# A fused attention and MLP kernel on one core: its 1722 jobs emitted in another order, with the PSUM banks dealt anew

## The chip, the cores and the metric

The kernel runs on one core of one Trainium2 chip. The metric is the device time of one execution, in microseconds (us), as the median of several runs. Inputs and outputs lie in the chip's memory; the kernel reads about 38 MB and writes about 17 MB there, most of it its own scratch.

## What is computed

One input `x` of 2048 tokens by 512 columns goes through a layer norm, and three things are added: `x` itself, an attention over four segments of 512 tokens with a memory carried from segment to segment, and a two-layer MLP on the normed tokens.

```python
xn = layernorm(x)
for s in range(4):                       # 32 heads of 16 columns; q, k, v = xn @ wq, wk, wv
    p = softmax(qs @ ks.T / 4 + mask)    # causal inside a segment
    a_dot = p @ vs
    a_mem = (phi(qs) @ M) / (phi(qs) @ z + 1e-6)      # phi(t) = t + 1 if t > 0 else exp(t)
    out_s = g * a_mem + (1 - g) * a_dot               # g = sigmoid(beta), one number per head
    M += phi(ks).T @ vs;  z += sum(phi(ks))
y = gelu(layernorm(xn) @ w1 + b1) @ w2 + b2           # 512 -> 1792 -> 512
return x + concat(out_s) @ wo + y
```

## The kernel before, in words

Matrices are split into a high and a low float16 half, and a product is made of three matmuls (high by high, high by low, low by high); the attention weights stay in float32. The work is cut into small jobs, each a short Python function that issues a few instructions on one to four engines. Sixteen units `i` (four segments times four groups of eight heads) and sixteen half-blocks `j` of the MLP run through them:

- front: `X` loads and norms a pair of token tiles (`ln`, L535, L549), `Xt` turns it on TensorE and splits it (`ln_out`, L564 to L568), `W` is a filler of two matmuls on the identity (`warm`, L500) that nobody reads, and `wl`, `wm`, `wf`, `ws` load the weights, measure their size (L353 on ScalarE, L382 as a trace on TensorE with L384 on VectorE), make power-of-two scales from that (L396, L414 and small VectorE steps) and split them (L447 and L448, or L450, L452, L454). `Cb` writes a row of ratios out of the norms (L527).
- `T` projects q or k of a unit (L586) and `V` the values (L586); the halves go through scratch memory to the layout that the scores need (`Tr`, L646).
- `M` makes scores and their row maxima (L740 on TensorE, L747 on VectorE), ten jobs a unit. `R` (`m_row`, L753) turns the 128x32 table of maxima `mc` on TensorE, ScalarE and VectorE split it into `mhl` (L755, L756), and SyncE's queue writes it to `md` (L758) and reads it back as two more rows of `qst` (`Rr`, L763).
- `S` makes the scores once more with the maxima subtracted by those rows (L782), ScalarE takes the exponential (L789) and GpSimd masks it (`Sg`, L803); `pv` and `PV` multiply by the values (L816); `O` divides (six steps).
- `N`, `K`, `Z`, `Q`, `Qt` keep the memory (L651, L717, L681, L696), `D` is the first MLP product (L586 with w1, L884), `G` the gelu (L891), `H` its split (L901, L903, L905), `e` the second product (L931, L935), `out` the output product (L951, L953), `st` the store (L864), `A` the loads of the accumulators (L909, L913).

TensorE works in three tilings: the whole 128x128 array (most jobs), two halves of 64 rows that work side by side (`M` and `S`), and four strips of 32 columns (`pv`, `PV`, `K`). `R` is a float32 transposition whose stationary operand `mc` has 32 columns, so its matmul is written with a 128x32 tile too.

What sets the order: nothing is scheduled at run time or by the compiler. A string of letters, `ORDER`, names for every step the stream from which the next job is taken, and the jobs are issued in that order; each engine works off its own instructions in the order in which they were issued, and waits by semaphores for what it needs. A second string, `BANKS`, names which of the eight PSUM banks each product is written to:

```python
banks = iter("".join(BANKS))
def dense():
    return dps.tile([P, 512], F32, name="dense" + next(banks), bufs=1)

for c in "".join(ORDER):
    key = next(todo[NAMES.index(c)])
```

A bank is taken again only when the last reader of what it held is done. Both strings were written by a search outside the kernel.

## Time and profile before

| | us |
|---|---|
| median of 3 runs | 690.41 (689.52 to 692.23) |
| span of the profiled execution, first to last instruction | 690.7 |
| TensorE busy, share of the span | 680.1, 98% |
| VectorE busy | 498.9, 72% |
| ScalarE busy | 471.4, 68% |
| GpSimd busy | 346.4, 50% |
| first matmul, end of the last matmul, after the span's start | 1.4, 687.0 |

The profiled execution's span and the median of the runs differ by 0.3 us. A timeline row gives a start, a duration, the engine, the line and operation, and the tiles as out<-in; `x6` are six instructions of the same kind, so the time from the start of one row to the start of the next is what the row cost its engine. Matmuls overlap, so a row's own duration is longer than that.

### The profile page before, as it was taken

To read this page: it belongs to the slowest core of one execution; us is meant where nothing else is said; L and a number is where in the kernel's file an instruction comes from. 1 tells how busy PE (TensorE), PEld (TensorE's weight loads), DVE (VectorE), ACT (ScalarE), POOL (GpSimd) and SP (SyncE) were. 2 spreads that over 40 slices of the span, in tenths; PEclk is the share of its full clock that TensorE was granted. 3 is DMA by queue.
4 is the path that set the end of the run, shared out by engine and by line. 5 is a ranking of instruction groups with operands and counts; after the bars stand their busy time and mean duration, and the time that the engine had idled before them with its cause. 6 is when DMAs were issued, how large, how long until landed. Compare 5 with 4: busy or idle time off the path is not lost.

```text
span 690.7 us, 15732 instructions
## 1 busy us (share of the span) xinstructions
PE 680.1 (98%) x5787; PEld 394.6 (57%) x5787; DVE 498.9 (72%) x1613; ACT 471.4 (68%) x877; POOL 346.4 (50%) x574
## 2 busy tenths in 40 slices
PE   8999999999999999999999999999999999999997
PEld 6764565656644565665555555566565446565543
DVE  5789888986796669676695875878468565787622
ACT  4578898897765578578836838556956554777960
POOL 5576587663525444373545344534372425365652
PEclk9999999999999999999999999999999999999999
DMA  9788433203320342312222133231411222420101
GB/s 267 230 199 218 113 91 105 79 2 91 81 49 16 87 108 55 95 47 72 70 70 57 31 79 86 57 85 39 99 35 56 69 65 61 107 65 2 33 1 61
DMA packets 52889, 55.83 MB, mean 81 GB/s; under 512 B 4990, under 2 KB 41868, under 8 KB 52812
## 3 DMA queue, kind: packets, MB, share of 16 engines
q1 hardware_dynamic: 50508, 50.64, 26.8%
q0 software_dynamic: 2304, 4.20, 3.8%
q8 instruction: 45, 0.74, 0.5%
q14 instruction: 32, 0.26, 0.1%
HBM read 37.77 MB, written 17.05 MB: 79 GB/s over the span
## 4 chain that ended last, share of the span: by engine, by line
PE 87%; DVE 8%; DMA 2%; issue 1%; SPq 1%; POOL 1%; ACT 0%; DVEq 0%
PE dense L586 35%; PE dense L931 20%; PE dense L816 10%; PE dense L951 6%; PE dense L782 6%; PE dense L740 5%; DVE dense L747 4%; PE dense L681 2%; PE dense L696 1%; DVE mc L747 1%; PE dense L564 1%; DMA pt<-in_A_wv_dram 1%; PE dense L651 1%; DMA qst<-md 1%; PE dense L382 0%
## 5 line engine op out<-in xcount | busy, mean ns | idle before, releaser
L747 DVE CUSTOM_DVE_ANT_0 dense<-dense,mask 128x384 f32<-128x384 f32 (+3 forms) x512 | 234.0, 528 | 33.9 <-PE dense L740 33.6
L789 ACT ACTIVATE pt<-dense,qkcs 128x512 f32<-128x512 f32 (+1 forms) x384 | 204.2, 628 | 46.3 <-PE dense L782 46.2
L931 PE MATMUL dense<-w2s,hT 128*128 128x512 f16 x672 | 166.3, 380 | 0.2 <-DVE hT L884 0.2
L586 PE MATMUL dense<-xnT,w1s 128*128 128x256 f16 x1344 | 160.2, 273 | 0.3 <-DVE mc L747 0.3
L803 POOL TENSOR_SCALAR_AFFINE_SELECT pt<-pt 128x256 f32<-128x256 f32 x256 | 99.4, 422 | 108.2 <-ACT pt L789 107.8
L586 PEld LDWEIGHTS <-w1s 128*128 128x128 f16 x1344 | 129.6, 98 | 29.1 <-issue 6.2
L905 POOL TENSOR_TENSOR hT<-hh,hT 128x512 f16<-128x512 f32 x64 | 67.6, 1057 | 83.6 <-ACT hT L903 70.4
L931 PEld LDWEIGHTS <-hT 128*128 128x128 f16 x672 | 61.3, 98 | 68.6 <-issue 13.4
L816 PE MATMUL dense<-pt,vt 128*32 128x512 f32 (+3 forms) x1024 | 78.0, 436 | 0.0
L747 DVE DVE_READ_ACCUMULATOR2_ANT mc<- 128x1 f32 x512 | 74.2, 145 | 0.0
L884 DVE SCALAR_TENSOR_TENSOR hT<-dense,sc,cb 128x512 f32<-128x512 f32 x64 | 43.5, 680 | 33.8 <-PE dense L586 25.2
L847 POOL TENSOR_TENSOR nN<-nN,oT 128x512 f32<-128x512 f32 x16 | 20.9, 1308 | 73.9 <-DVE oT L663 73.9
L901 POOL TENSOR_SCALAR hh<-hT,sc 128x512 f32<-128x512 f32 x64 | 42.5, 664 | 24.1 <-ACT hT L891 15.5
L816 PEld LDWEIGHTS dense<-pt,vt 128*32 128x32 f32 x1024 | 31.1, 109 | 40.7 <-issue 29.4
L782 PE MATMUL dense<-qst,kst 50*128 50x384 f16 (+3 forms) x512 | 52.1, 299 | 1.8 <-DMA qst<-md 1.8
L740 PE MATMUL dense<-kst,qst 48*128 48x384 f16 (+3 forms) x512 | 52.2, 298 | 0.0
L891 ACT ACTIVATE hT<-hT,b1t 128x256 f32<-128x256 f32 x112 | 47.0, 496 | 5.0 <-DVE hT L884 4.6
L903 ACT ACTIVATE hT<-hh 128x512 f16<-128x512 f32 x64 | 37.3, 583 | 14.9 <-POOL hh L901 14.9
L951 PE MATMUL dense<-wos,oT 128*128 128x512 f16 (+2 forms) x204 | 44.0, 367 | 0.8 <-DVE acc L953 0.7
L586 PE MATMUL dense<-xnT,wks 128*128 128x512 f16 (+1 forms) x252 | 44.5, 329 | 0.2 <-DVE mc L747 0.2
L586 PE MATMUL dense<-xnT,wqs 128*128 128x512 f16 (+1 forms) x252 | 44.2, 329 | 0.1
L586 PE MATMUL dense<-wvs,xnT 128*128 128x512 f16 x192 | 43.9, 379 | 0.1
(227 smaller groups left out, 832.0 us busy)
## 6 DMA issues: line engine op xcount, KB each, us to landing
kst<-kd SPq DMA_DIRECT2D x32, 192.0 KB
qst<-qd SPq DMA_DIRECT2D x32, 192.0 KB
qd<-hl SPq DMA_DIRECT2D x36, 128.0 KB
kd<-hl SPq DMA_DIRECT2D x33, 128.0 KB
acc<-in_A_x_dram SPq DMA_DIRECT2D x16, 256.0 KB
acc<-in_B_b_dram POOLq DMA_DIRECT2D x16, 256.0 KB, 4.2
out_dram<-acc SPq DMA_DIRECT2D x15, 256.0 KB
xt<-in_A_x_dram SPq DMA_DIRECT2D x14, 256.0 KB
```

The source lines that it names most:

```text
L586: T.matmul(p, ws(k, a), xs(k, b), start=i == 0, stop=i == 3 * KT - 1)
L740: T.matmul(p[:, o:o + n], stk[i, 0][r, t, P * qb:P * qb + P], stk[i, 1][r, t, :n], start=True, stop=True)
L747: V.tensor_tensor_reduce(p[:, o:o + n], p[:, o:o + n], mask[:, 512 - n:], 1.0, -3e38, OP.add, OP.max, mc[i][:, 4 * b + t, qb:qb + 1])
L782: T.matmul(p[:, o:o + n], stk[i, 1][r, t, P * kb:P * kb + P], stk[i, 0][r, t, P * kb:], start=True, stop=True)
L789: A.activation(pt[i, 4 * b + t][:, OFF[kb]:OFF[kb] + n], p[:, c:c + n], AF.Exp, scale=qkcs[:, 1, i % NG:i % NG + 1])
L803: G.affine_select(v, v, pattern=[[0, 2], [1, P]], compare_op=OP.is_ge, fill=0.0, base=0, channel_multiplier=-1)
L816: T.matmul(p[32 * c:32 * c + 32, P * kb:], vt[s, kb][:, 4 * g + c, 16 * odd:16 * odd + 32], pt[i, 2 * c + odd][:, OFF[kb]:OFF[kb] + LEN[kb ...
L884: V.scalar_tensor_tensor(hz[:, f0:f + 1, :], p[:, :256 * n].rearrange("p (f c) -> p f c", f=n), col(CG + fh), cbt[hf].unsqueeze(1).to_broa ...
L891: A.activation(hz[:, f, :], hz[:, f, :], AF.Gelu_apprx_tanh, bias=b1t[:, fo:fo + 1])
L905: G.tensor_tensor(hT[:, z, 1, :], hht[j, c], hT[:, z, 0, :], op=OP.subtract)
L931: T.matmul(p, t[:, u, P * a:P * a + P], w2s[:, fo, v, :], start=fi == 0 and n == 0, stop=fi == FH - 1 and n == 2)
L951: T.matmul(p[:, c], o[:, u, P * b:P * b + P], wos[:, g, v, c], start=i == 0, stop=i == 3 * NG - 1)
```

## The change

`ORDER` and `BANKS` are replaced; not a job is added, removed or altered. The strings have the same lengths (1722 jobs, 964 products that take a bank). The new order comes from a search that charges every change of TensorE's tiling.

```diff
 ORDER = (
-    "auhhwhhhlkhhkhhbth6xc6khldlhhie$hfhhhhkjhx6f78$hhahhv$rg7%%8%k8%h8bR8cs8mRde8i&ff9m9gj9n&!n&#y&z((CA)9*(CD+(+2"
...
+    "ahukhhhkhtbhhlslclhdeh6ihh6khjfh6hahfhhwkhh$h$v87$7%bcrhxmk%gh8g8ih%d%eRfmfR888$&8nxhCnj&9&9y&z()A((*DC!((+XDX"
...
 BANKS = (
-    "01234567012345670123460123647013654701542670546173250641732570641257106457106457103645120365412306524306512430"
...
+    "00000000000001223334444455670011233467346675146370254136702541736254130625413062541306254730564273526743502764"
...
 )
```

What that does to the engines' queues is shown at three places.

The first is TensorE where unit 0's maxima are turned (L753, the job `R`). In the old program the rows around it are these (L586 is the MLP's first product, L931 its second, L414 the sum of a weight's size; the many equal rows between are left out):

```order
L586 MATMUL dense_960<-xnT,w1s 128x256
...
L931 LDWEIGHTS hT_126
L931 MATMUL dense_858<-w2s,hT_126 128x512
...
L753 MATMUL dense_1001<-ident,mc 32x128
...
L414 MATMUL dense_1021<-am,ones 128x4
```

And in the new one (L717 is the memory's product, job `K`, in strips of 32 columns; L740 the scores of unit 1, in halves of 64 rows):

```order
L931 MATMUL dense_845<-w2s,hT_126 128x512
L717 MATMUL dense_996<-vt_84,pkn 32x32 x4
L717 MATMUL dense_996<-vt_85,pkn 32x32 x4
L717 MATMUL dense_996<-vt_86,pkn 32x32 x4
L717 MATMUL dense_996<-vt_87,pkn 32x32 x4
L753 MATMUL dense_1014<-ident,mc 32x128
L740 LDWEIGHTS qst_89
L740 MATMUL dense_1030<-kst_91,qst_89 128x512
```

`R` stood inside work on the whole array, and now stands between a job in column strips and one in row halves. Of the sixteen `R`, eight now follow a job in column strips and one a job in row halves; before, all sixteen followed a job on the whole array. Counted over the whole of both programs, by the tile that each matmul is written with, the tiling changes 298 times before and 282 times after. With `R` counted as work on the whole array it changes 266 times before and 270 times after.

The second place is SyncE's queue around the same step: `md` is the write and the read-back of the maxima, `oT` the last two pieces of w2, `rc` and `ame` pieces of w1. Before:

```order
L310 DMA rc<-in_B_w_dram 128x4x128
L310 DMA ame<-in_B_w_dram 128x4x128
L646 DMA kst_91<-kd_93 48x4x512 x2
L646 DMA qst_89<-qd_95 48x4x512 x2
L758 DMA md_96<-mhl 32x2x128
L312 DMA oT<-in_B_w_dram 128x512 x2
L763 DMA qst_88<-md_96 2x2048 x2
```

After:

```order
L646 DMA kst_91<-kd_93 48x4x512 x2
L646 DMA qst_89<-qd_95 48x4x512 x2
L310 DMA rc<-in_B_w_dram 128x4x128
L310 DMA ame<-in_B_w_dram 128x4x128
L312 DMA oT<-in_B_w_dram 128x512 x2
L758 DMA md_96<-mhl 32x2x128
L763 DMA qst_88<-md_96 2x2048 x2
```

The half megabyte for `oT` was issued between the write of the maxima and their read-back, and is now issued ahead of the write.

The third place is VectorE at the front, where it splits the first weights (L448), sums the trace of wv (L384) and takes the sums of the second pair of token tiles (L474, L475). Before:

```order
L448 SCALAR_TENSOR_TENSOR wks<-wks,qksc 128x512
L384 SCALAR_TENSOR_TENSOR dense_217,am<-dense_217,ident 128x128
L978 COPY gr<-zr 128x32
L981 TENSOR_TENSOR zr<-zr,half 128x8 x4
L982 TENSOR_REDUCE bet<-zr 128x4
L388 TENSOR_SCALAR dense_316<-dense_316 128x1
L392 TENSOR_SCALAR sc<-dense_316 128x1 x2
L975 COPY b1t<-dense_321 128x14
L448 SCALAR_TENSOR_TENSOR wqs<-wqs,qksc 128x512
L448 SCALAR_TENSOR_TENSOR wvs<-wvs,sc 128x512 x2
L448 SCALAR_TENSOR_TENSOR wvs<-pt,sc,wvs 128x512 x2
L474 BN_STATS st<-nN 128x6
```

After:

```order
L384 SCALAR_TENSOR_TENSOR dense_273,am<-dense_273,ident 128x128
L978 COPY gr<-zr 128x32
L981 TENSOR_TENSOR zr<-zr,half 128x8 x4
L982 TENSOR_REDUCE bet<-zr 128x4
L448 SCALAR_TENSOR_TENSOR wks<-wks,qksc 128x512
L388 TENSOR_SCALAR dense_307<-dense_307 128x1
L392 TENSOR_SCALAR sc<-dense_307 128x1 x2
L448 SCALAR_TENSOR_TENSOR wqs<-wqs,qksc 128x512
L448 SCALAR_TENSOR_TENSOR wvs<-wvs,sc 128x512
L474 BN_STATS st<-nN 128x6
L475 BN_AGGR ag<-st 128x2
L474 BN_STATS st<-nD 128x6
```

The low half of wk now stands behind the trace of wv, and the sums of the second pair of tiles stand ahead of three of the four low halves of wv. At the same time the fillers before TensorE's first other matmul go from 26 matmuls to 24, that first matmul is the ratio row (L527) where it was the trace of wv (L382), and SyncE loads wk and wq ahead of wv.

## The prediction, on record before the changed kernel ran

> **What bounds the kernel now.** I read the page first, then the windows by stage, then who TensorE waited for, and last TensorE's timeline. The page's first lines and three windows (us of the stretch, then busy us of each engine, granted clock, DMA share) settle where the time is:

> ```profile
> span 690.7 us, 15732 instructions
> PE 680.1 (98%) x5787; PEld 394.6 (57%) x5787; DVE 498.9 (72%) x1613; ACT 471.4 (68%) x877; POOL 346.4 (50%) x574
> 75.00:200.00 125.00, 124.75 (x1183) 74.85 (x1182) 105.56 (x334) 106.12 (x199) 74.95 (x127) 1.00 0.29 72
> 200.00:400.00 200.00, 199.73 (x1770) 115.42 (x1772) 148.50 (x490) 132.84 (x246) 93.92 (x163) 1.00 0.24 62
> 400.00:660.00 260.00, 259.84 (x2116) 145.61 (x2109) 177.76 (x577) 172.97 (x321) 121.76 (x197) 1.00 0.25 62
> ```

> From 75 to 660 us TensorE is idle 0.25 + 0.27 + 0.16 = 0.7 us. The other engines have room (VectorE's fullest stretch is 105.56 of 125). Since the same matmuls run after the change, three things alone can move the end: what TensorE pays between matmuls when its tiling changes, the idle time at both ends, and new waits in the middle. The view of TensorE's waits (total, times, longest) has one that is longer than a start or a tail, in the first scores of unit 0:

> ```profile
> PE dense L782 <- DMA qst<-md: 1.8, 2, 1.3
> ```

> **Term 1, the changes of tiling.** Their price is read from starts on TensorE's timeline (start, duration, then what):

> ```profile
> 60.76 0.81 PE L931 MATMUL dense<-w2s,hT 128*128 128x512 f16 x3
> 61.41 0.27 PE L753 MATMUL dense<-ident,mc 128*32 128x128 f32 x1
> 61.52 0.81 PE L931 MATMUL dense<-w2s,hT 128*128 128x512 f16 x3
> 62.16 0.28 PE L414 MATMUL dense<-am,ones 128*128 128x4 f32 x2
> 62.30 1.46 PE L931 MATMUL dense<-w2s,hT 128*128 128x512 f16 x6
> 63.60 0.60 PE L651 MATMUL dense<-ident,phk 128*128 128x128 f32 x4
> 64.03 0.81 PE L931 MATMUL dense<-w2s,hT 128*128 128x512 f16 x3
> 64.78 0.61 PE L740 MATMUL dense<-kst,qst 48*128 48x512 f16 x6
> 65.32 2.12 PE L931 MATMUL dense<-w2s,hT 128*128 128x512 f16 x9
> 67.84 0.39 PE L782 MATMUL dense<-qst,kst 50*128 50x512 f16 x1 [0.41 <-DMA qst<-md]
> 69.57 0.39 PE L782 MATMUL dense<-qst,kst 50*128 50x512 f16 x1 [1.35 <-DMA qst<-md]
> ```

> Three L931 cost 0.65 us (60.76 to 61.41) where more work on the whole array follows, 0.217 us each, and 0.75 us (64.03 to 64.78) where row halves follow: a change costs 0.75 - 0.65 = 0.10 us, 0.095 with the trace's finer digits. Column strips are no different:

> ```profile
> 320.33 1.46 PE L931 MATMUL dense<-w2s,hT 128*128 128x512 f16 x6
> 321.72 2.14 PE L816 MATMUL dense<-pt,vt 128*32 128x512 f32 x24
> ```

> Six L931 need 6 x 0.217 = 1.30 us and took 1.39, so 0.09 us into strips. But the first three rows above show more: the transposition of the maxima (L753, written as 128*32) begins 0.65 us after the three L931, with nothing added, and the L931 behind it begins 0.11 us later, which is what other 128-column float32 transpositions cost (four L651 in 63.60 to 64.03, 0.108 each). L753 costs no change: to TensorE it is work on the whole array. Counted so, the changes go from 266 to 270, not from 298 to 282, and term 1 is +4 x 0.095 = +0.4 us. The new order puts `R` behind column strips eight times, a neighbourhood that the old trace does not show. Should strips pass into `R` and on to the whole array free of charge, eight changes vanish, and 262 stay: -4 x 0.095 = -0.4 us. I take +0.4, since the rows that are there all treat `R` as whole-array work; ends -1.5 and +0.4.

> [...]

> **Term 2, the first scores of unit 0.** In the rows above the nine L931 end at 65.32 + 9 x 0.217 + 0.095 = 67.36. The first L782 starts 0.48 us late, its partner, which would follow within 0.01 us, 1.73 us after it: 2.2 us lost. The chain of waits and SyncE's queue say why:

> ```profile
> 62.72 2.63 DMA md<-mhl
> 65.67 3.85 DMA qst<-md
> ```

> ```profile
> 62.72 0.30 SPq L758 DMA_DIRECT2D md<-mhl  x1
> 63.07 2.00 SPq L312 DMA_DIRECT2D oT<-in_B_w_dram  x2
> 65.36 0.57 SPq L763 DMA_DIRECT2D qst<-md  x2
> ```

> The read-back of 16 KB took 3.85 us with 512 KB of w2 just in front of it. After the change that half megabyte goes out before the write of the maxima. Against this, TensorE has less to do meanwhile. From L753 to the place of the first L782 it had 67.36 - 61.41 = 5.95 us. Now it has, from the rows above, L753 0.11, a change 0.095, two M jobs with the change out of them 0.54 (64.78 to 65.32), six `e` jobs at 0.65, L414 0.14, N 0.43, a change and one M 0.31: 5.53 us. A later round, with the queue quiet, shows what is enough:

> ```profile
> 408.05 0.27 PE L753 MATMUL dense<-ident,mc 128*32 128x128 f32 x1
> 413.45 0.82 PE L782 MATMUL dense<-qst,kst 50*128 50x512 f16 x8
> ```

> There 5.40 us sufficed without a wait. At 60 us weights still flow, so I leave 0.8 us of the 2.2: -1.4 us. Ends: -2.2 (nothing left), and +0.5 (0.4 us of cover gone, the transfers no faster).

> **Term 3, the front.** Four idle stretches before 36 us carry names on TensorE's timeline; the first is the cold start, which stays.

> ```profile
> 1.42 5.73 PE L500 MATMUL dense<-ident 128*128 128x256 bf16 x26 [1.42 <-POOL ident masks.py:199]
> 7.58 0.63 PE L382 MATMUL dense<-wvs 128*128 128x128 bf16 x8 [0.42 <-DMA wvs<-in_A_wv_dram]
> 11.66 0.40 PE L382 MATMUL dense<-pt 128*128 128x128 bf16 x4 [0.48 <-DMA pt<-in_A_wv_dram]
> 12.39 0.40 PE L382 MATMUL dense<-pt 128*128 128x128 bf16 x4 [0.34 <-DMA pt<-in_A_wv_dram]
> 13.95 1.48 PE L586 MATMUL dense<-xnT,wks 128*128 128x256 f16 x12
> 16.18 2.75 PE L586 MATMUL dense<-wvs,xnT 128*128 128x512 f16 x12
> 33.14 1.47 PE L586 MATMUL dense<-xnT,w1s 128*128 128x256 f16 x12
> 35.61 0.38 PE L414 MATMUL dense<-am,ones 128*128 128x1 f32 x2 [1.00 <-DVE dense L384]
> ```

> They idle 0.42 + 0.48 + 0.34 + 1.00 = 2.2 us, and with the last matmul's tail that runs out ahead of each, about 0.2 us, 3.0 us are lost. In the new order the waits for wv should go, as it has 24 filler matmuls, the first pair's turn and seven more filler jobs ahead of it. But others come. 24 fillers at 0.22 us (5.73 / 26) end near 6.7 us, and the ratio row comes next, whose GpSimd chain ended at 8.09 + 0.19 = 8.3 us:

> ```profile
> 8.09 0.19 POOL L514 TENSOR_TENSOR stats<-stats 128x2 f32<-128x2 f32 x1
> ```

> With GpSimd's large memsets moved behind that chain I put its end at 8.0: a wait of 1.3 us. VectorE then carries more ahead of the first V job:

> ```profile
> 13.07 0.29 DVE L384 SCALAR_TENSOR_TENSOR dense<-dense,ident 128x128 f32<-128x128 f32 x1
> 16.71 1.41 DVE L448 SCALAR_TENSOR_TENSOR wvs<-pt,sc,wvs 128x512 f16<-128x512 f32 x2
> 18.04 0.69 DVE L474 BATCH_NORM_STATS2 st<-nN 128x6 f32<-128x512 f32 x1
> 19.55 0.18 DVE L475 BATCH_NORM_AGGREGATE ag<-st 128x2 f32<-128x6 f32 x1
> 21.59 0.53 DVE L535 TENSOR_SCALAR nD<-nD,ag,stats 128x512 f32<-128x512 f32 x1
> ```

> From L384 at 13.07 to the last low half of wv at 18.0 are 5 us; the sums of the second pair (18.04 to 19.7, 1.7 us), one L535 (0.5) and one wk half (0.7) join it, 2.9 us. The q projection of 1.3 us, now ahead of V, and two pieces of trace and filler cover part; I leave 1.0 us at the first k projection and V together. The first D job (33.14) loses cover as well: between the scale of w1 and it stood T (1.3), T of unit 1 (2.6) and both traces of w2 (1.6), with waits 5.9 us; now T of unit 1 and one trace, 3.5 us, against a preparation on VectorE, GpSimd and ScalarE that I put at 4.3: 0.7 us. The last wait (1.2) I leave at 0.3, as two D jobs more lie ahead of it. Sum 1.3 + 1.0 + 0.7 + 0.3 = 3.3 against 3.0: +0.3 us; ends -1.5 (the half of the old waits goes, little comes) and +2.5.

> **Term 4, the middle and the tail.** A new order can starve TensorE anywhere between 75 and 660 us. By the same sums of rows the covers are alike in both orders: from `R` to the first `S` of a unit the shortest are 5.3 before and 5.4 after, from `S` to `pv` 2.8 and 2.8, from the last D to the first `e` of a half-block, the front's first aside, 17.3 and 16.0. Nothing there is shorter than what sufficed, by more than half a microsecond. I take 0, ends -1.0 and +1.5. The last jobs (`e`, then four `out`) are the same, 0.

> **Sum.** +0.4 - 1.4 + 0.3 + 0 = -0.7 us on the profiled 690.7, and so on the median, 0.3 us lower: 690.4 - 0.7 = 689.7. No measurement of this kernel tells less than about 0.5%, 3.45 us, from no change: 686.95 to 693.85.

> **Rivals.** (a) The charge works as written: every change by the written tile, -1.5 us in place of +0.4 makes the sum -2.6: 687.8. Against it stand the rows at 60.76 to 61.52; inside 0.5% all the same. Chance 0.15. (b) Faster by over 0.5%: the wait for the maxima goes wholly (-2.2) and the front keeps only 1.5 of its 3.0 (-1.5), with the eight free changes (-0.4): 690.4 - 4.1 = 686.3. For it speaks that wk, wq and wv are all loaded sooner; against it VectorE's and GpSimd's longer lists at the front. Chance 0.12. (c) Slower: the preparation of weights becomes the bound before 40 us. It decides if the low halves of wv and the first of w1 are late by the whole of what was put ahead of them: 2.9 us at V and 2.4 (5.9 - 3.5) at D, with 1.3 at the ratio row and none of the old waits saved but the 1.1 of wv: +5.5, less 1.4 from term 2, plus 0.4: 694.9. For it speaks that V began at 16.18 while VectorE made its last halves until 18.1, so V had no slack. Chance 0.12. My forecast has the remaining 0.61.

> **Range and chances.** The forecast's own ends come from terms that do not err together: about -2.5 to +3.0, so 687.2 to 692.7, which holds (a). Drawn out to (b) below and by half a microsecond above, 686.3 to 693.2 leaves out (c) and little else. Faster by over 0.5% is (b), 0.12; slower is (c), 0.12; the rest, 0.76, is within 0.5%.

> **What would show it.** Right: spacing of 0.31 us from an L931 to row halves as now, and 0.2 us from the last L717 or L816 to L753 where a strip job precedes it (a free change would show 0.11 or less); L782 waiting for qst<-md under 1 us near 68 us; the ratio row L527 waiting for GpSimd near 8 us; the first M near 44 us, as in the old trace. Wrong: more than 2 us of TensorE idle between 75 and 660 us, or the first M more than 2 us off.

## The result, and the profile after

The changed kernel takes 710.66 us (median of 4 runs) against 690.82 us: a ratio of 1.030, interval 1.0271 to 1.0328. It is slower by 20 us, and lies 21 us above the forecast of 689.7 us. The profiled execution took 709.83 us with a span of 708.1 us, where the old one's span was 690.7. In every execution on record the time is 1.7 us longer than the span, so the old profiled execution was a long one of its kernel (an estimate: 690.7 + 1.7 = 692.4 us). Of 52 later executions of the old kernel 6 had a span of 690.7 us or more, and their median is 688.9. That is most of why the two traces below are 17.4 us apart and not 20.

The page's first lines and the same three windows (us, busy us of each engine with instructions, granted clock, DMA share, GB/s):

```profile
span 708.1 us, 15687 instructions
PE 690.8 (98%) x5787; PEld 395.9 (56%) x5787; DVE 504.4 (71%) x1613; ACT 470.8 (66%) x877; POOL 353.8 (50%) x574
75.00:200.00 125.00, 122.92 (x1157) 74.18 (x1156) 103.11 (x332) 106.84 (x203) 78.41 (x128) 1.00 0.30 76
200.00:400.00 200.00, 199.55 (x1730) 114.44 (x1729) 146.33 (x478) 133.34 (x248) 91.17 (x155) 1.00 0.26 67
400.00:660.00 260.00, 256.23 (x2084) 143.41 (x2083) 185.36 (x603) 163.94 (x306) 118.24 (x192) 0.99 0.25 61
```

TensorE's share still reads 98%, with its busy time 10.7 us up for the same matmuls: time at half clock counts as busy (from 51.82 to 55.23 us busy for 3.41 of 3.41 us at a granted clock of 0.50, with 14 matmuls), and so does most of the time that a matmul is held up behind another (from 4.03 to 7.44 us busy for 3.13 of 3.41 us with 12 filler matmuls; the old kernel's stretch from 3.64 to 7.05 has 17). Between 75 and 660 us TensorE is now idle for 2.1 + 0.4 + 3.8 = 6.3 us, where it was 0.7. Whom TensorE waited for (total, times, longest) has new names at the top:

```profile
PE dense L740 <- DMA qst<-qd: 4.1, 6, 1.2
PE dense L586 <- POOL w1s L454: 1.7, 2, 1.3
PE dense L500 <- POOL ident masks.py:199: 1.4, 1, 1.4
PE dense L782 <- DMA qst<-md: 1.4, 2, 0.9
PE dense L586 <- DVE wvs L448: 1.2, 1, 1.2
```

Where the lag grows is read from TensorE's timelines at the first M job of a unit (which jobs lie ahead of it differs a little between the orders):

| place | before, us | changed, us | behind, us |
|---|---|---|---|
| first M of unit 0 | 43.81 | 50.85 | 7.0 |
| first M of unit 4 | 176.08 | 185.88 | 9.8 |
| first M of unit 12 | 507.71 | 522.84 | 15.1 |
| end of the span | 690.7 | 708.1 | 17.4 |

**The front, 7.0 us.** TensorE's timeline of the changed kernel (start, duration, what, and in brackets the idle time and what ended it):

```profile
1.42 7.65 PE L500 MATMUL dense<-ident 128*128 128x256 bf16 x24 [1.42 <-POOL ident masks.py:199]
9.22 0.66 PE L527 MATMUL dense<-ident,stats 128*128 128x128 f32 x2
...
11.44 0.81 PE L500 MATMUL dense<-ident 128*128 128x256 bf16 x4
12.31 0.66 PE L564 MATMUL dense<-ident,xt 128*128 128x128 f32 x4
...
24.96 0.59 PE L586 MATMUL dense<-wvs,xnT 128*128 128x512 f16 x2 [1.22 <-DVE wvs L448]
...
40.16 1.27 PE L586 MATMUL dense<-xnT,w1s 128*128 128x256 f16 x10 [0.20 <-DVE w1s L448]
...
42.71 1.26 PE L586 MATMUL dense<-xnT,w1s 128*128 128x256 f16 x10 [0.39 <-POOL w1s L454]
...
49.58 1.26 PE L586 MATMUL dense<-xnT,w1s 128*128 128x256 f16 x10 [1.31 <-POOL w1s L454]
```

The old kernel's timeline where fillers run at full clock:

```profile
8.70 1.04 PE L500 MATMUL dense<-ident 128*128 128x256 bf16 x8
9.57 0.38 PE L527 MATMUL dense<-ident,stats 128*128 128x128 f32 x2
```

The named waits, with one of 0.22 us near 16 us, are 3.3 us in place of 2.2, only 1.1 more. The rest is in the fillers (L500). Eight filler matmuls of the old kernel take 0.87 us (8.70 to 9.57), and so do four of the new one (11.44 to 12.31). The difference is in the first row of the new `BANKS`: the first twelve fillers all have bank 0, and several of the later ones share a bank with the job next to them. The second of two such jobs starts 0.22 us late at full clock (at 11.55 us the last matmul of a job starts, at 11.88 the next job; fillers otherwise follow every 0.11 us). It leaves TensorE idle for only 0.06 us, and the timeline names idle times from 0.15 us on; but the trace's semaphores name whom it waits for, and that is TensorE itself. In this front 20 jobs start 0.04 us after the semaphore that the last matmul of the job before raises at its end. In the old kernel's front there is none. The 24 matmuls at the start end at 9.07 us and not at 6.7 (2.4 us), the clock rises at 10.86 us and not at 7.05 as in the old trace (0.9 us for the work from 9.07 on), and nine later jobs at or behind a filler pay 0.22 us each (2.0): about 5 of the 5.9 us. The rise of the clock is read from the matmuls' spacing, 0.213 us for 256 columns before it and 0.109 after; the windows' clock column shows 1.00 ahead of the first change on record.

**Behind the first M, 10.4 us.** The last read-back of q rows shows the kind. TensorE, and SyncE's queue:

```profile
634.28 0.39 PE L740 MATMUL dense<-kst,qst 48*128 48x512 f16 x1 [1.19 <-DMA qst<-qd]
635.03 0.55 PE L740 MATMUL dense<-kst,qst 48*128 48x512 f16 x4 [0.36 <-DMA qst<-qd]
...
636.01 4.18 PE L931 MATMUL dense<-w2s,hT 128*128 128x512 f16 x12
```

```profile
619.89 0.57 SPq L627 DMA_DIRECT2D qd<-hl  x1
...
621.55 0.93 SPq L646 DMA_DIRECT2D kst<-kd  x2
629.23 0.30 SPq L758 DMA_DIRECT2D md<-mhl  x1
629.65 0.87 SPq L646 DMA_DIRECT2D qst<-qd  x2
```

The q rows were written at 619.89 us, but their read-back stands in SyncE's queue behind the write of unit 14's maxima, which SyncE issued only at 629.23. Then the twelve L931 behind the wait take 4.18 us (2.76 in a_queue, below). Two windows say why (the granted clock is the third number from the right):

```profile
51.82:55.23 3.41, 3.41 (x14) 1.75 (x15) 3.05 (x15) 3.35 (x9) 2.67 (x3) 0.50 1.09 353
635.50:638.91 3.41, 3.41 (x11) 1.05 (x9) 2.24 (x10) 2.75 (x4) 1.56 (x2) 0.50 0.04 13
```

After two of the longer waits TensorE was granted half its clock for 3.41 us. From the spacings of all matmuls: waits for q rows of units 0, 2, 7, 12 and 15 cost 5.5 us (none before), the two drops of the clock 3.2, waits for maxima 1.9 (2.0 before), four changes of tiling 0.4. That makes 9.0 of the 10.4 us; the rest is in steps too small to name. This is the account of one execution. Another of the four had a granted clock of 1.000, so no drop behind its first rise (an estimate: one of 3.41 us at 0.50 would take 0.002 from the mean), and took 709.88 us all the same; what it lost in their place isn't known, since it was not profiled.

### The profile page after: what moved, and what is told of

Read it like the earlier page. It is cut to its first block, busy times and chain, and to the rows that moved or that the text cites. A ratio compares the mean times of both kernels' runs of the same rounds, so it can differ in the third digit from the quotient of the medians.

```text
span 708.1 us, 15687 instructions
## 1 busy us (share of the span) xinstructions
PE 690.8 (98%) x5787; PEld 395.9 (56%) x5787; DVE 504.4 (71%) x1613; ACT 470.8 (66%) x877; POOL 353.8 (50%) x574
## 4 chain that ended last, share of the span: by engine, by line
PE 76%; DVE 8%; DMA 7%; ACT 5%; issue 2%; POOL 2%; SPq 0%; POOLq 0%; ACTq 0%; DVEq 0%
PE dense L586 28%; PE dense L931 16%; PE dense L816 9%; PE dense L951 6%; PE dense L782 5%; PE dense L740 5%; DMA qst<-qd 4%; DVE dense L747 2%; PE dense L681 1%; PE dense L500 1%; ACT pt L789 1%; PE dense L564 1%; DMA qst<-md 1%; DMA qd<-hl 1%; ACT hT L891 1%
## 5 line engine op out<-in xcount | busy, mean ns | idle before, releaser
L931 PE MATMUL dense<-w2s,hT 128*128 128x512 f16 x672 | 169.0, 382 | 0.1
L586 PE MATMUL dense<-xnT,w1s 128*128 128x256 f16 x1344 | 160.6, 273 | 1.9 <-POOL w1s L454 1.7
L586 PEld LDWEIGHTS <-w1s 128*128 128x128 f16 x1344 | 129.2, 98 | 31.7 <-issue 5.9
L931 PEld LDWEIGHTS <-hT 128*128 128x128 f16 x672 | 61.8, 98 | 66.4 <-issue 14.8
L816 PE MATMUL dense<-pt,vt 128*32 128x512 f32 (+3 forms) x1024 | 78.2, 436 | 0.2 <-POOL stats L491 0.2
L747 DVE DVE_READ_ACCUMULATOR2_ANT mc<- 128x1 f32 x512 | 71.3, 139 | 0.0
L740 PE MATMUL dense<-kst,qst 48*128 48x128 f16 (+3 forms) x512 | 54.7, 301 | 4.7 <-DMA qst<-qd 4.1
L816 PEld LDWEIGHTS dense<-pt,vt 128*32 128x32 f32 x1024 | 31.4, 109 | 42.5 <-issue 29.8
L782 PE MATMUL dense<-qst,kst 50*128 50x384 f16 (+3 forms) x512 | 53.0, 299 | 1.5 <-DMA qst<-md 1.4
L586 PE MATMUL dense<-xnT,wks 128*128 128x512 f16 (+1 forms) x252 | 45.2, 331 | 0.3 <-DVE xnT L568 0.2
L586 PE MATMUL dense<-wvs,xnT 128*128 128x512 f16 x192 | 43.9, 379 | 1.3 <-DVE wvs L448 1.2
L951 PE MATMUL dense<-wos,oT 128*128 128x512 f16 (+2 forms) x204 | 43.8, 367 | 0.8 <-DVE acc L953 0.7
L586 PE MATMUL dense<-xnT,wqs 128*128 128x512 f16 (+1 forms) x252 | 44.4, 328 | 0.0
L935 DVE SCALAR_TENSOR_TENSOR acc<-dense,sc,acc 128x512 f32<-128x512 f32 x32 | 23.9, 746 | 24.1 <-PE dense L931 17.9
```

The lines of the kernel that those rows point to most:

```text
L586: T.matmul(p, ws(k, a), xs(k, b), start=i == 0, stop=i == 3 * KT - 1)
L740: T.matmul(p[:, o:o + n], stk[i, 0][r, t, P * qb:P * qb + P], stk[i, 1][r, t, :n], start=True, stop=True)
L747: V.tensor_tensor_reduce(p[:, o:o + n], p[:, o:o + n], mask[:, 512 - n:], 1.0, -3e38, OP.add, OP.max, mc[i][:, 4 * b + t, qb:qb + 1])
L782: T.matmul(p[:, o:o + n], stk[i, 1][r, t, P * kb:P * kb + P], stk[i, 0][r, t, P * kb:], start=True, stop=True)
L816: T.matmul(p[32 * c:32 * c + 32, P * kb:], vt[s, kb][:, 4 * g + c, 16 * odd:16 * odd + 32], pt[i, 2 * c + odd][:, OFF[kb]:OFF[kb] + LEN[kb ...
L931: T.matmul(p, t[:, u, P * a:P * a + P], w2s[:, fo, v, :], start=fi == 0 and n == 0, stop=fi == FH - 1 and n == 2)
```

## Experiments

All ratios are to the kernel before, run on the same chip. A job's name is its key: `W` a filler, `Tr,i,0` the read-back of unit i's q rows, `M` and `S` the two rounds of scores, `R` and `Rr` write and read-back of the maxima, `X` and `C` sums and ratio, `ws` and `wl` preparation and load of a weight.

### The fillers' banks

```diff
 a_fill_rot: the changed kernel, BANKS of W_0 to W_23 alone (20 of them differ)
-0 0 0 0 0 0 0 0 0 0 0 0 2 3 3 4 4 4 4 5 0 1 3 6
+0 1 2 3 4 5 6 7 0 1 2 3 4 5 6 7 0 1 2 5 3 2 4 6
 b_fill_one: the kernel before, BANKS of W_0 to W_23 alone
-0 1 2 3 4 5 6 7 0 1 2 3 4 6 0 1 2 3 6 3 6 4 7 5
+0 0 0 0 0 0 0 0 0 0 0 0 0 6 7 7 7 7 4 5 5 5 5 5
```

> The changed kernel with its order kept and only the banks of 23 of the 24 filler jobs dealt anew, so that no filler writes the bank of the TensorE job just before it. Theory F (fillers on one bank): in the changed kernel a filler job on the bank of the job before it takes 0.64 us in place of 0.43 while the clock is low and waits 0.22 us once it is high, and the later end of the fillers brought the rise of the clock from 7.05 to 10.86 us. Then the clock should rise near 7 us, the first M job come 4 to 6 us earlier (near 45 to 47 us), and the time be 704.5 to 706.5 in place of 710.7, a ratio to the kernel before of 1.020 to 1.023. Rival G (the preparation of weights on VectorE and GpSimd sets the front): what the fillers give comes back as longer waits for wvs and w1s, the first M job moves by less than 1.5 us, and the time stays at 709 to 710.5, ratio 1.026 to 1.029.

Measured: 707.61 us, ratio 1.0234 (1.0201 to 1.0267), between the two theories. The first M job comes at 48.81 us, 2.0 earlier. TensorE's timeline and two windows of this run:

```profile
1.43 4.35 PE L500 MATMUL dense<-ident 128*128 128x256 bf16 x24 [1.43 <-POOL ident masks.py:199]
8.16 0.69 PE L527 MATMUL dense<-ident,stats 128*128 128x128 f32 x2 [2.39 <-POOL stats L514]
```

```profile
4.64:8.06 3.42, 1.13 (x10) 0.77 (x8) 1.72 (x4) 1.03 (x3) 2.24 (x7) 1.00 0.86 274
8.06:11.47 3.41, 3.31 (x17) 3.00 (x18) 1.06 (x6) 1.39 (x4) 1.04 (x5) 0.50 0.94 303
```

The fillers now end at 5.8 us, 3.3 us earlier, so F has their price right. But the ratio row then waits 2.39 us for GpSimd, and behind that idle time the clock is halved from 8.06 to 11.47 us. The slow fillers had hidden a wait.

> The kernel before with its order kept and only the banks of its fillers changed: the first 13 on bank 0, the later ones on the bank of the TensorE job just before them where that one is free. Theory F: the first 26 filler matmuls end near 8.3 us in place of 7.15, the clock rises later, and the time grows by 3 to 5.5 us, to 694 to 696 (ratio 1.004 to 1.008). Rival G: the old waits for wv (1.24 us) and of the later front (1.7 us) take up the delay, and the time grows by 0 to 1.5 us (ratio 1.000 to 1.002).

Measured: 701.14 us, ratio 1.0144 (1.0117 to 1.0170): 10 us, twice what F expected, and rival G is out. The first M job comes at 53.55 us, 9.7 late. The window shows what F had left out:

```profile
14.73:24.97 10.24, 8.53 (x46) 6.18 (x44) 5.50 (x24) 4.16 (x7) 0.00 (x0) 0.50 1.15 314
```

The clock rises at 11.31 us, and falls again from 14.73 to 24.97, after a wait of 1.41 us and eight fillers that took 1.52 us (13.06 to 14.58) where the old kernel's take 0.87. A string of banks that touches nothing but idle-time fillers costs 1.4% of the kernel.

### All banks dealt by one rule

In these two, `ORDER` is kept and every entry of `BANKS` is the bank that has been free longest.

> The changed kernel's order with all 964 tiles of PSUM given the bank that has been free longest. If the fillers are all that the dealing of banks did wrong, this equals the changed kernel with the fillers alone dealt anew, within 1 us (704.5 to 706.5 by theory F, 709 to 710.5 by rival G). If other banks of the changed kernel cost time too (rival H), it is faster than that one by over 1 us, and TensorE's small waits after 45 us shrink.

> The control: the kernel before with its order kept and all PSUM banks dealt by the same rule, longest free first. Both F and G: within 1 us of the kernel before, ratio 0.9985 to 1.0015, since its own banks already rotate at the front. If the rule itself costs or gains more, the comparison of the two orders under one rule has to be read against this run.

Measured: a_lru 712.44 us, ratio 1.0314 (1.0290 to 1.0338); b_lru 699.83 us, ratio 1.0125 (1.0110 to 1.0140). The control failed: the rule itself costs the old order 9 us. In b_lru, where the longest wait is:

```profile
469.53 0.63 PE L681 MATMUL dense<-mx,phq 128*128 128x136 f32 x4
472.83 0.79 PE L681 MATMUL dense<-mx,phq 128*128 128x136 f32 x4 [2.67 <-ACT pt L789]
```

A bank that is free by the order of emission is not yet free in time: here it still waits for ScalarE's exponential. So these runs can't compare the orders. One thing they do show: with its fillers apart and no drop of the clock at the front, the new order's first M job comes at 47.03 us. Of the front's 7.0 us 3.8 were the fillers and the clock, net of what they hid, and 3.2 the order.

### Which part of the order

Each of these takes one order up to a certain job and then the other order's remaining jobs; each job keeps its own kernel's banks (new fillers as in a_fill_rot).

> The order of the kernel before up to its first M job, then all other jobs in the changed kernel's order; each tile keeps the bank of the kernel whose order its job follows. Theory R (the rest of the new order has its own waits: q rows that come late, md, and the drops of the clock behind them): the first M job comes near 43.8 us as before, the waits for q rows near units 2, 12 and 15 stay, and the time is 699 to 702, ratio 1.012 to 1.016. Rival I (the waits of the middle are inherited from the late front, through transfers and VectorE work pushed into each other): the middle runs as in the kernel before, 691 to 694, ratio 1.000 to 1.005.

> The other half: the changed kernel's order up to its first M job, with the fillers' banks dealt so that none follows itself, then all other jobs in the order and the banks of the kernel before. Theory R: only the front's own loss is left, 3.2 us for the longer waits of ratio row, wv and w1 (and up to 2 more if the clock falls behind the ratio row): the first M job at 47 to 49 us, the time 694 to 696, ratio 1.0045 to 1.0075. Rival I: 700 or more, with waits for q rows in the middle.

Measured: h_bfront_arest 706.49 us, ratio 1.0234 (1.0189 to 1.0279); h_afront_brest 699.44, ratio 1.0114 (1.0083 to 1.0144). Both lie above what R expected. In the profiled executions the seam has its own price: 2.4 us for a bank at 52.4 us with half clock for 6.8 us behind it in the one, 2.6 us at 70.9 us with 3.4 us of half clock in the other. The first of these executions was the longest of its four (712.85 us). Of the second kernel's four, the two with a granted clock of 1.000 took 696.6 and 698.2 us, near R's 694 to 696, and the two with 0.995 and 0.993 took 700.7 and 701.4. The waits of the middle stayed where the new order's rest is (qst<-qd near units 2, 12 and 15), and are missing where the old one's is, which speaks for R. A seam in a calmer place was to settle it:

> The order of the kernel before up to the first M job of unit 4 (176 us there, 186 in the changed kernel), then the changed kernel's order. From that job to the end the kernel before takes 514.6 us and the changed kernel 522.2. If the later part has its own loss (theory R: the waits near 300, 466, 522 and 634 us with a half clock behind the last), the time is 696.5 to 700.5, ratio 1.008 to 1.014. If it is inherited from the first part (rival I), 690.5 to 693, ratio 1.000 to 1.004.

> The changed kernel's order, its fillers' banks dealt apart, up to the first M job of unit 4 (183.6 us in that kernel, 176.1 in the kernel before), then the order of the kernel before. Theory R: the first part's loss alone, 7.5 us, 696.5 to 700, ratio 1.008 to 1.013. Rival I: as much as the changed kernel with those fillers, 705 or more. If this and its counterpart add up to less than 1.015 together, a part of the loss comes only from the two meeting.

Measured: h_b4_arest 702.93 us, ratio 1.0185 (1.0154 to 1.0216); h_a4_brest 707.73, ratio 1.0245 (1.0231 to 1.0259), both above R's range, and the second inside rival I's (705 or more). Again there are seams: 2.9 us in the first, 3.8 us and 6.8 us of half clock in the second, near 186 us. So the totals don't decide, but the traces behind the seams do. From the first M of unit 4 (176.83 us) to the end (699.0) the profiled h_b4_arest takes 522.2 us, as the changed kernel does, though it gets there 9 us earlier. Its waits at unit 15:

```profile
626.19 0.39 PE L740 MATMUL dense<-kst,qst 48*128 48x512 f16 x1 [1.30 <-DMA qst<-qd]
626.98 0.55 PE L740 MATMUL dense<-kst,qst 48*128 48x512 f16 x4 [0.41 <-DMA qst<-qd]
```

These are the changed kernel's 1.19 and 0.36 us. And from the first M of unit 5 (218.78 us) to the end (706.1) h_a4_brest takes 487.3 us, where the kernel before takes 487.7 (203.01 to 690.7), though it gets there 15.8 us later. Rival I falls: behind the seam each order runs as it does in its own kernel, so each part of the new order has its own loss. The two ratios add up to 4.3% where the whole costs 3.0%, so the parts can't be priced by these runs better than to a few microseconds.

### Mending the new order

```diff
 a_queue, two jobs moved in the changed order
-  ... R_14 ... Tr_15_0 ... Rr_14        ... Rr_6 ... Tr_7_0 ... M_7_0
+  ... Tr_15_0 R_14 ... Rr_14            ... Tr_7_0 Rr_6 ... M_7_0
 a_prep, with a_fill_rot's banks
-  X_0_1_1 X_0_1_2 ... C_1 ... ws_v_2_0 X_0_1_3 ws_v_3_0 X_0_1_4
+  ... ws_v_2_0 ws_v_3_0 X_0_1_1 X_0_1_2 X_0_1_3 X_0_1_4 C_1
-  ws_2a_0_0 ws_QK_0_2 ... ws_1a_6_1 ... ws_1a_6_2
+  ws_1a_6_1 ws_1a_6_2 ws_2a_0_0 ws_QK_0_2
-  Cb_0 Xt_0_0_0 ... Xt_0_0_1
+  Xt_0_0_0 ... Xt_0_0_1 Cb_0
 a_cover, a_queue's moves with a_fill_rot's banks, and
+  Tr_0_1 Tr_0_0 right behind Tv_1_0;  Rr_10 ahead of Tr_11_1
+  M_2_0 M_2_1 behind pv_1_0_2;  M_10_0 behind e_8_0_3
+  e_10_1_5 e_10_1_6 D_12_4 ahead of M_12_0;  e_9_0_4 D_10_5 ahead of S_10_0
 a_fix: a_prep and a_cover together
```

> The changed kernel with two jobs moved: the read-back of unit 15's q rows goes ahead of the write of unit 14's maxima, and unit 7's ahead of the read-back of unit 6's maxima. Theory Q (a read-back stands in SyncE's queue behind an issue that waits for other work): the waits near 634 us (1.8 us) and 300 us (0.5) go, and with the first the half clock of 635.5 to 638.9 us (1.6 us): 3 to 4 us faster than the changed kernel, 706.5 to 708, ratio 1.0225 to 1.0245. Rival L (the rows themselves or their transfer come late): the waits stay within 0.3 us, and the time is 710 to 711.

Measured: 710.11 us, ratio 1.0272 (1.0247 to 1.0297), not told apart from the changed kernel. The profile shows the mechanism right and the sum given back. TensorE at the same place as above:

```profile
636.28 0.61 PE L740 MATMUL dense<-kst,qst 48*128 48x512 f16 x6
637.04 0.62 PE L782 MATMUL dense<-qst,kst 50*128 50x512 f16 x2 [0.16 <-DMA qst<-md]
637.60 2.76 PE L931 MATMUL dense<-w2s,hT 128*128 128x512 f16 x12
```

The wait is gone, and the twelve L931 run at full clock. From the first M job to the end it takes 654.0 us in place of 657.2, which is theory Q's price, though a new wait of 1.2 us for q rows has come up at unit 10 (437 us). But in this execution the clock rose at 18.84 us, not at 10.86, with the front untouched, and the first M job came at 54.06 us, 3.2 us late. At unit 7, 0.3 of the 0.5 us stayed.

> The changed kernel with the fillers' banks dealt apart, and eight jobs of the front moved: the sums of the second pair and its ratio chain behind the last low half of wv, the last parts of w1's seventh piece ahead of a part of w2 and of wk, and the ratio row behind the first pair's second turn. Theory P (the front's loss is the order in which VectorE and GpSimd prepare): the waits of the ratio row (2.4 us), of V (1.7) and of the last D job (1.3) fall to under 0.6 us together, the first M job comes at 44.5 to 46 us in place of 48.8, and the time is 703.5 to 705.5, ratio 1.018 to 1.021. Rival D (what TensorE gains there it loses at the next read-back, whose transfers do not move): the waits for the q rows of unit 0 grow by over 2 us, and the time stays at 706 to 708.

> The changed kernel with the fillers' banks dealt apart, and the places mended at which TensorE waits for a read-back after 50 us: read-backs of units 0, 7 and 15 and of unit 10's maxima moved ahead in SyncE's queue, the first M jobs of units 2, 10 and 12 and the first S job of unit 10 moved behind one to three jobs that are ready. Theory Q: these waits (7 us with the half clock behind two of them) fall to under 2 us, and the time to 699 to 702, ratio 1.012 to 1.016. Rival E (the new order has no slack anywhere: what is mended returns as another wait): the sum of TensorE's idle time after 50 us falls by less than 2 us, and the time is 705 or more.

> Both sets of moves together. By P and Q together the changed order has then nothing left against the kernel before but four more changes of tiling (0.4 us) and some 2 us of small waits: 692 to 697, ratio 1.003 to 1.009. By D or E: 700 or more.

Measured: a_prep 708.81 us, ratio 1.0254 (1.0225 to 1.0283); a_cover 709.84, ratio 1.0282 (1.0250 to 1.0314); a_fix 706.31, ratio 1.0228 (1.0211 to 1.0246). Against a_fill_rot (1.0234) none gains anything that its interval shows. P, Q and their sum are wrong as prices. TensorE's timeline of a_prep:

```profile
21.39 0.63 PE L564 MATMUL dense<-ident,nN 128*128 128x128 f32 x4 [1.55 <-DVE nN L535]
...
46.37 0.39 PE L740 MATMUL dense<-kst,qst 48*128 48x512 f16 x1 [1.00 <-DMA qst<-qd]
47.30 0.82 PE L740 MATMUL dense<-kst,qst 48*128 48x512 f16 x7 [0.54 <-DMA qst<-qd]
...
57.65 0.77 PE L740 MATMUL dense<-kst,qst 48*128 48x384 f16 x5 [0.83 <-DVE mc L747]
...
60.06 2.75 PE L586 MATMUL dense<-wvs,xnT 128*128 128x512 f16 x12 [0.88 <-DVE phk L638]
```

The last D job's wait is gone and the first M job comes 2.4 us earlier than in a_fill_rot. But V's wait became one for the second pair's rows (their sums now come later), the q rows of unit 0 are late instead (1.5 us idle in place of 0.3, as rival D has it, though not by over 2), and behind them stand waits for banks that VectorE has not read. a_cover removed the waits for q rows at units 2, 7, 12 and 15, and got others. In a_fix, where both sets stand:

```profile
51.71 0.81 PE L931 MATMUL dense<-w2s,hT 128*128 128x512 f16 x3 [1.00 <-ACT pkn L653]
...
60.01 4.11 PE L586 MATMUL dense<-wvs,xnT 128*128 128x512 f16 x12 [0.87 <-DVE phk L638]
...
522.80 0.39 PE L782 MATMUL dense<-qst,kst 50*128 50x512 f16 x2 [1.50 <-DVE mc L747]
```

Not one of these is a read-back: they are banks that ScalarE or VectorE still holds (the last at a place that a_cover's own move made), and the second row shows a drop of the clock as well (12 L586 in 4.11 us, 2.75 in a_prep). This is rival E: TensorE's named idle time behind 50 us is 8.7 us in a_fill_rot, 7.7 in a_cover and 7.3 in a_fix. What remains after 50 us was not traced further.

### The same kind of step in the old order

```diff
 b_md, one job of the old order moved
-  ... wl_2b_1 ws_1b_0_0 e_0_0_6 Rr_0
+  ... ws_1b_0_0 e_0_0_6 Rr_0 wl_2b_1
 b_front, two jobs moved;  b_wf, only the second of them
-  wl_QK_0 W_10 wl_v_1
+  wl_v_1 wl_QK_0 W_10
-  wf_2a D_0_1
+  D_0_1 wf_2a
```

> The kernel before with one job moved: the load of half a megabyte of w2 from in front of the read-back of unit 0's maxima to behind it. Theory M (that load stood in the way, as term 2 has it): the two waits for qst<-md near 68 and 70 us, 2.0 us together, fall to under 0.5 us, and the time by 1.5 to 2.0 us, to 689.0 to 689.4, ratio 0.997 to 0.998. Rival N (the round through DRAM takes that long anyway, or the load of w2 is now late for its matmuls): waits of over 1.2 us stay, at the same place or at w2, and the time is within 0.7 us of the kernel before.

> The kernel before with two jobs moved: the trace of w2 that TensorE waits for at 35.6 us (1.0 us) behind one D job, and the load of the second half of wv ahead of that of wk's and wq's second halves (waits of 0.48 and 0.34 us). If both waits simply go, the first M job comes 1.0 to 1.8 us earlier and the time is 689.0 to 690.0, ratio 0.997 to 0.999, faster than both kernels. If they only move (to w1's first pieces, or to the q rows of unit 0), it is within 0.5 us of the kernel before.

> The kernel before with one job moved: the trace of w2 (L414, waited for at 35.6 us, 1.0 us) behind one D job, and the load of wv left where it was. If the wait goes, it is 0.7 to 1.2 us faster than the kernel before, ratio 0.998 to 0.999. If it moves to the D job's weights, or to the maxima of unit 0 near 68 us, less than 0.4 us.

Measured: b_md 691.80 us, ratio 1.0005 (0.9991 to 1.0019); b_front 689.77, ratio 0.9987 (0.9970 to 1.0004); b_wf 690.48, ratio 1.0002 (0.9991 to 1.0013). In b_md the wait for qst<-md is gone, as M has it, and the same scores wait 1.7 us at 71.2 us for ScalarE's exponentials, with a granted clock of 0.50 behind it, from 71.40 to 74.82 us: no gain, but not by N's reason. In b_front and b_wf the wait at 35.6 us is gone and so is the one for the maxima near 68 us, with 2.2 and 2.4 us less of span than the old profiled execution. But the medians move by 0.5 and 0.2 us only, since that old execution was itself a long one: against the median span of 688.9 us the two are 0.4 and 0.6 us shorter. What b_front's other move was for did not come: the waits for weights ahead of the traces grew from 1.2 to 1.7 us. b_front is the lowest version of all, and not told apart from the kernel before.

## Why the prediction was wrong, point by point

**What bounds the kernel: right, and not used to the end.** TensorE bound the old kernel with 0.7 us idle in 585. In such a program a new wait can go straight into the time, and the prediction looked for them at too few places. Both of its own signs of being wrong came: 6.3 us idle between 75 and 660 us, and the first M 7.0 us late.

**Term 1 held.** In the changed kernel:

```profile
70.03 0.81 PE L931 MATMUL dense<-w2s,hT 128*128 128x512 f16 x3
70.77 0.46 PE L717 MATMUL dense<-vt,pkn 128*32 128x32 f32 x32
71.16 0.29 PE L753 MATMUL dense<-ident,mc 128*32 128x128 f32 x1
71.38 0.61 PE L740 MATMUL dense<-kst,qst 48*128 48x512 f16 x6
...
77.48 0.84 PE L782 MATMUL dense<-qst,kst 50*128 50x512 f16 x6 [0.47 <-DMA qst<-md]
```

The 32 strips need 0.39 us up to L753, against 0.28 in the old trace where more strips follow (its row at 95.05 us), and L753 needs 0.22 up to the row halves, its own 0.11 and a change. So `R` is work on the whole array also behind strips, the changes are 270, and rival (a) is out. The -1.5 us in it and in the term's lower end (16 changes fewer by the written tile, at 0.095 us each) no run shows; the rows above give four changes more, +0.4 us. At 0.4 us the term was never what decided.

**Term 2 held where it looked.** The wait near 68 us became one of 0.64 us in all (0.47 idle) at 77.48 us; 0.8 was forecast. But the new order has a like wait of 1.2 us at unit 10 (466 us), which no term counted. The base was also doubtful: the prediction took the span of 690.7 us and the median time of 690.4 for nearly the same thing, while the traced execution was some 2 us longer than the median one. How much of the 2.2 us near 68 us a usual execution loses no run shows, and b_front and b_wf, without that wait, gain almost nothing on the median.

**Term 3 failed in its first sentence of costs:** "24 fillers at 0.22 us each (5.73 / 26) end near 6.7 us". The price came from fillers on rotating banks, though the diff of the change shows the new `BANKS` beginning with a row of zeros. The fillers ended at 9.07 us, the clock rose 3.8 us later than in the old trace, and b_fill_one shows that a like edit alone costs the old kernel 10 us. The other parts were right in kind: with the fillers apart (a_lru) the ratio row waits 1.55 us (1.3 forecast), k and V 1.8 (1.0), the first D jobs 0.6 (0.7), the last D job 1.3 (0.3). These 5.2 us against 2.2 before make 3.0, nearly the 3.2 us that a_lru's first M job is late; the forecast was 0.3. Rival (c), preparation as the bound, thus had the right mechanism at about half the price, as one part of three.

**Term 4 failed:** "by the same sums of rows the covers are alike in both orders". They were, for the three covers that were summed. The one for the q rows was not among them: from the issue of their read-back to the first M job the old trace never has less than 4.9 us, the new one has 3.9 to 5.0 in five units. Even that cover doesn't settle where TensorE waits, since the trip itself varies. Units 6 and 10, with 3.9 and 4.0 us, did not wait. Units 7, 12 and 15 did, with 4.9 to 5.3 us from the issue to the landing in the chain that ended last, and so did units 0 and 2, where the landing took 6.5 and 6.2 us. Nor was SyncE's queue read for what stands ahead of each read-back, as it was in term 2 for one of them. And the sums were TensorE's alone: at unit 10 the cover of the maxima is 5.6 us, more than the 5.40 that had sufficed, but VectorE had 1.4 us of other steps to do before it could split them. And no term had a price for the granted clock, which turned about 1.8 us of wait into about 3.5 at unit 15.

**What stays open.** That the loss sits in both the front and the rest is shown by the four exchanged orders, and that the fillers' banks carry a part of it (3 us of the 20, a_fill_rot) by the bank runs. That the waits named here are the whole cause is not, nor that a repaired order would reach the old time: a_fix kept 16 of 20 us, in waits that took the place of those mended.

## What to carry to other kernels

Before pricing a new order of a program whose bottleneck engine is never idle, list every producer and consumer pair that goes through another engine or a queue, DRAM round trips first, and read each one's cover and what stands ahead of it in its queue. Read the table of buffers or banks as closely as the order: a string that only says where fillers write cost the old order 10 us. And price the granted clock with the wait: at unit 15 of the changed kernel 1.8 us of waiting cost TensorE about 3.5, with the clock at 0.50 for the 3.41 us behind it.

## What the runs showed of the hardware that was not expected

Both traces can be cut into pieces of 3.41 us at those multiples. In the pieces ahead of the two drops in the middle of the changed kernel TensorE was busy for 1.70 us (48.40 to 51.82) and 1.87 us (632.08 to 635.50), the latter with 1.19 and 0.36 us of wait in it. Of the pieces at full clock behind which it stayed full, the least busy had 2.41 us in this trace (464.83 to 468.24) and 2.33 in the old one (68.49 to 71.90). In a_fill_rot, b_md, b_fill_one and a_fix stretches of that length ahead of a drop had 1.13, 1.74, 1.84 and 2.19 us. The busy time alone doesn't settle it: a_queue, whose mean granted clock is 1.000, has a stretch with 2.12 us (523.95 to 527.40). What decides a drop or a rise is not shown. The first rise came at 10.86 us in one execution and at 18.84 in another of the same front (a_queue), in both with the first twelve fillers on one bank. In a_fill_rot the times go with the granted clock: 704.5 us at 1.000, 706.3 at 0.997, and 709.0 and 709.3 at 0.995.

**A bank written twice in a row.** A filler on the bank of the TensorE job before it starts 0.22 us late at full clock (0.64 us a job in place of 0.43 at half clock). The trace shows a wait of the program for it: the job starts on the semaphore that TensorE raises at the end of the job before, in 20 places of the changed kernel's front and in none of the old kernel's. With the fillers' banks apart (a_fill_rot) eight fillers take 0.88 us at full clock (11.68 to 12.56), in the changed kernel 1.74 (12.81 to 14.55). What the bank would cost without that wait is not shown.
